# Linear attention beside a Mish layer: query exponentials normalized before they are turned, numerators without zero blocks, one load of key and value weights, a new order of steps

## Chip, cores and metric

One core of a Trainium2 chip runs the whole program. The metric is the time of one execution on the device in microseconds; 151.07 is the median of three runs of the kernel before. The engines are named as in the profile: PE (matmuls) with PEld (its weight loads), ScalarE (ACT), VectorE (DVE), GpSimd (POOL) and SyncE (SP), which here only issues DMA transfers. Each engine works through its own queue in program order and waits on semaphores of the others.

## What is computed

2048 tokens of width 448 are layer-normalized; the result goes through two branches, which are added to the input.

```python
xn = layernorm(x)
# branch A: 16 heads of width 28
q, k, v = heads(xn @ wqkv)
pq, pk = q @ w_phi, k @ w_phi                     # per head, 28 x 28
phi_q = concat(softmax(pq), softmax(-pq))         # 56 features
phi_k = concat(softmax(pk), softmax(-pk))
kv  = phi_k.T @ v                                 # per head, 56 x 28
z   = phi_k.sum(over tokens)
num = phi_q @ kv
den = phi_q @ z + 1e-6
a = heads_joined(num / den) @ wo
# branch B
h = xn @ w1 + b1                                  # width 1792
b = (h * tanh(softplus(h))) @ w2
out = x + a + b                                   # bf16
```

## The kernel before

The tokens stand in 16 tiles t of 128, worked on in 8 pairs u = t // 2. The program is a list of named steps, the table ORDER; a step appends instructions to the queues of one or more engines, and the class Program puts in the waits. The order of the table is therefore the order on each engine. The steps:

- `l...` load: x tiles (`lx0` to `lx6`), key weights (`lkm`), value weights (`lvm`), both their last 64 rows twice (`lkt`), query weights transposed by DMA (`lqT0` to `lqT3`), then `l1m`, `l1t` (W1), `l2` (W2), `lo` (Wo). Almost all go through SP's queue.
- `z12` warms PE up with 12 matmuls on zeros (L364).
- `st`, `rs`, `xn`, `xt`: the layer norm of a pair: BN statistics on VectorE (L462, L464; with b the second tile's on ScalarE), 1/sqrt on ScalarE or GpSimd (L473), the normalized tile (L497, GpSimd L492), and its transpose xnT, by PE (L505) or by a DMA transpose.
- `wtk`, `wmk`, `wmq`: w_phi is multiplied into the key weights (transposed by PE, L556, then L580) and into the query weights. For the latter VectorE first doubles the last columns of WqT (`qd`, L286).
- `v`, `k`, `q`: the three products of a pair (L423), each cut into parts A, B (6 matmuls of 64 rows by 448 columns each) and H (2). Two row halves run side by side. v is copied out; k and q leave through two exponentials on ScalarE, exp(x) and exp(-x) (L618, L680).
- `kn`: key features of a pair and a sign are normalized: reduce (L626) and reciprocal (L628) on VectorE, multiply on GpSimd (L630).
- `e`: a tile of query exponentials, not normalized, is turned into EqT by a DMA transpose. There are three buffers for them: Eq0 and two rows of actT, which the feed-forward branch writes later.
- `kv`: 32 small matmuls of a pair add phi_k^T v into one bank (L649). `kvz` copies the sum to KVT (L660), in blocks with zeros between them, and a DMA transpose makes KVZ.
- `nd`: numerators and denominators of a tile: 16 matmuls of 60 columns (L722). A product's 60 columns hold for one sign and two heads both the sum over that sign's features and, from the column of ones beside v, z and the plain sum of the exponentials. VectorE copies the two plain sums (L738), multiplies each sign's numerator by the other's sum (L742, L744), adds (L746), takes the reciprocal (L748) and multiplies (L749).
- `ot`, `wo`: the result of a pair is turned by DMA and multiplied by Wo (L845).
- `f0`, `f1`: W1 for one block of 128 hidden units and half of the tokens, 14 matmuls of 512 columns (L423), left through Mish on ScalarE (L699). `g`: W2 for a tile, 14 matmuls of 448 columns (L828), then the addition to x (L793) and the stores `sto`, `stt`.

Products that live longer than one step hold two of the eight PSUM banks, a pair of banks; a pair is opened again after its last reader, mostly ScalarE, is done. Four such pairs are in use in turn.

Of the kernel before, what the change touches and what calls it, by code (L numbers as in the profile page):

```python
# [12 lines left out]
D = 448  # L13
# [7 lines left out]
G = 4  # L21
# [6 lines left out]
NDW = 2 * (DH + 2)  # L28
# [10 lines left out]
class Program:  # L39
# [4 lines left out]
    def __init__(self, nc, es):  # L44
        self.nc = nc
        self.es = es
        self.ops = {e: [] for e in self.ENGINES}
        self.writers = {}
        self.readers = {}
        self.psum = {}  # L50
        self.n_dma = 0

    def op(self, eng, fn, r=(), w=(), dma=False, tag="", after=()):
# [84 lines left out]

def bass_parallel_sum__linear_kernel_hedgehog__dense_activation_mish__prompt_kernel(
# [8 lines left out]
pv table lx2s lba zero pm st2b lx3s lkms lps st3b lkts z12 pi b1 rs2p pw rs3a xn2d bd lx1s wtk0b lvms lx4s xn3d xt2b  # L148
wtk1b wmk0b lqT2 xt3a v2Ha wmk1a v2Ba lqT0 st1 v3Ha lqT1 lqT3 rs1a v3Aa v2Aa st4 rs4p pk v3Ba k3H lx0s k3A qd xn1d
wmq0d wmq1a k2H k3B lx6s pp k2A st5 q3A xn4d k2B q3B rs5p q2A xt1m l1ts q3H k1A q2H xn5p xt4m st0 v1Ad k1H st6 xt5m e7  # L150
rs0p q2B st7 xn0d v1Bd k1B v1Hd rs7p rs6p k4A k4H q1B k4B xn6d q1H q1A v4Ad k5H xn7d v4Hd k5A v4Bd v5Ad kn1.0 xt0m k5B
v5Bd k0B xt6m v5Hd xt7m v0Ba kn2.1 kn2.0 k0H k0A e3 k6H k6A kn0.0 e2 v6Ba l1ms k6B v0Ha kn0.1 v0Aa v6Aa v6Ha k7H k7A
q4B e6 k7B v7Aa v7Ha kn7.0 q4H q4A q6A q6H v7Ba e9 q6B kn6.0 f0.2B kn5.1 f0.0A f1.2A f0.2A f0.0H f1.2H kn6.1 e5 f1.3B
f0.2H f0.0B e12 f1.2B f1.3A kn4.1 f0.3B kn5.0 f1.3H e13 f0.3H f0.1B e4 f0.3A f0.1H f0.1A q7H q0A kn3.1 q0H kn4.0 q5B
e8 q0B q7B kv5 kn7.1 e0 kv0 kv2 q7A q5A f0.13A q5H f0.13B kv7 kv4 e10 kv6 f0.13H f0.6H f0.6A kn3.0 f0.10A f0.6B kn1.1
f0.10B kv3 kv1 ep f0.10H f1.7H f1.7A e11 f1.9A kvz f1.7B f0.12B f1.5B f0.12A f1.5H f0.5H f1.9H f0.12H l2s f1.9B f1.5A
f0.5A f1.1A nd3 f1.1B f0.5B e15 f1.0A f1.1H f1.13B f1.0H f1.13H f1.0B nd2 los f1.13A ot1m f1.8B f0.9H f1.8A f1.8H nd0
f0.11B f0.9A f0.11A f0.11H f0.7A f0.7H f0.8B nd6 e14 f0.8H f0.9B f0.7B e1 f0.8A f1.12H f1.12A f1.10A nd7 f1.10B f1.4H
f1.10H f1.12B ot3m f1.4A nd1 f1.6B f1.4B f0.4H f1.6A ot0m f0.4A wo1H f1.6H f0.4B nd4 wo1A wo3A wo1B wo3H nd5 ot2m g1
g3 g2 f1.11A f1.11H nd11 wo0B f1.11B wo3B wo0A nd13 wo0H nd10 g6 ot5m g0 g7 g11 nd12 wo2A wo5A sto1 ot6m wo5H wo2B  # L160
nd15 nd9 g10 sto0 g5 nd14 ot7m wo2H wo5B nd8 g4 g9 g14 g13 g12 g8 sto3 ot4m wo4H wo4A wo6B wo7B sto2 wo6H wo6A sto5
wo4B sto4 wo7H wob wo7A g15 stt14 sto6 stt15
# [8 lines left out]
def _kernel(es, nc, A_x, A_wqkv, A_w_phi, A_wo, B_w1, B_b1, B_w2, out):  # L171
# [43 lines left out]
    KVT = sb("KVT", [P, G, 2, 2, 64], BF16)  # L215
    KVZ = sb("KVZ", [P, 2 * G, P], BF16)
    rden = [sb(f"rden{i}", [P, H], FP32) for i in range(2)]
    Sq = [sb(f"Sq{i}", [P, 2, H], FP32) for i in range(2)]

    o_sb = [xn[i][:, :].rearrange("p (i d) -> p i d", i=2) for i in range(2)]  # L220

    def as_t(n):
        return v_flat[:, :].bitcast(FP32)[:, n * H * (DH + 1):(n + 1) * H * (DH + 1)].rearrange("p (h c) -> p h c", c=DH + 1)

    t1, t2 = [as_t(0), as_t(1)], as_t(2)
# [116 lines left out]
    def p_pads():  # L342
        for i in (1, 2, 0):
            op("POOL", lambda e, i=i: e.memset(Eq_of(i).rearrange("p i s (h n) -> p (i s h) n", n=64)[:, :, QP:64], 0.0),
               w=[("Eqp", i)] + ([(n, h) for n in ("WT", "WU") for h in range(2)] if i == 0 else []), tag=f"pp{i}")

    def p_kvt():
        op("POOL", lambda e: e.memset(KVT[:, :, :, :, :].rearrange("p g s x f -> p (g s x f)").bitcast(mybir.dt.uint32),
                                      0), w=[("KVT0",)], tag="pk3")

    def eps_rows():
        for i in range(2):
            op("DVE", lambda e, i=i: e.tensor_reduce(epsT[:, i:i + 1], ap_on(ident[:, DH + i:DH + i + 1], [[32, 4]]),
                                                          AX.X, ALU.add),
               r=[("ident",)], w=[("epsT", i)], tag=f"ep{i}")
        op("DVE", lambda e: e.scalar_tensor_tensor(epsT[:, 2:3], epsT[:, 0:1], DEN_EPS / 2, epsT[:, 1:2], ALU.mult,
                                                   ALU.add), r=[("epsT", 0), ("epsT", 1)], w=[("epsT", 2)], tag="ep2")
# [621 lines left out]
```

## Time and profile before

| | |
|---|---|
| time, median of 3 runs | 151.07 us (150.71 to 151.2) |
| profiled execution, span | 148.7 us, 3864 instructions |
| profiled execution, own time | not given beside the span |
| granted PE clock over the span | 1.000 |
| DMA traffic | 17.23 MB, mean 116 GB/s |

The page of a profile lists the busy time of each engine, then the span in 40 slices of 3.7 us with a digit of the busy share in tenths, then the chain that ended last, followed back from the last instruction to what released it. Groups of instructions are given as line, engine, operation, output from input, shape, count, then busy time in us, mean duration in ns, and the idle time of the engine before them with what ended it. A timeline or chain row begins with its start and its length in us.

### The profile page before, as it was taken

The page shows a single profiled execution, that of the slowest core. Times are in us where ns is not written, and L with a number is a line of the kernel's source. Part 1 is how long each engine was busy: PE and PEld are TensorE (multiplying, and loading weights), DVE is VectorE, ACT ScalarE, POOL GpSimd, SP SyncE. Part 2 cuts the span into 40 slices and gives each one's busy share as a digit, 9 for nine tenths or more (in the row PEclk, how much of TensorE's full clock was granted, in tenths as well). Part 3 has the DMA queues.
Part 4 walks back from the last instruction along what each step waited for, and adds up shares of the span by engine and source line. Part 5 has one row for each costly group of instructions (what it writes and reads, how often), then busy time and mean ns, then how long its engine had stood idle before and what let it go on. Part 6 is the DMA issues. An engine that isn't in the chain of part 4 may idle for free.

```text
span 148.7 us, 3864 instructions
## 1 busy us (share of the span) xinstructions
PE 144.0 (97%) x1669; PEld 74.2 (50%) x1669; DVE 102.7 (69%) x229; ACT 74.7 (50%) x91; POOL 38.9 (26%) x53
## 2 busy tenths in 40 slices
PE   6899999999999999999999999999999999999992
PEld 2365555555444555444444445545555555555561
DVE  0699898996999930407787989529983999930072
ACT  4997999779999999567747661002000000000000
POOL 4424465179999992000000000000000000000000
PEclk9999999999999999999999999999999999999999
DMA  4997997799699069499956053210013130551005
GB/s 131 245 278 216 119 185 149 126 170 344 103 188 196 14 52 132 85 239 295 195 98 125 4 62 62 43 23 0 7 37 86 35 93 0 123 127 58 4 10 175
DMA packets 39964, 17.23 MB, mean 116 GB/s; under 512 B 33932, under 2 KB 39180, under 8 KB 39948
## 3 DMA queue, kind: packets, MB, share of 16 engines
q1 hardware_dynamic: 39776, 16.89, 54.4%
q8 instruction: 13, 0.21, 0.6%
q10 hardware_dynamic: 172, 0.10, 0.2%
q14 instruction: 3, 0.02, 0.0%
HBM read 7.02 MB, written 1.84 MB: 60 GB/s over the span
## 4 chain that ended last, share of the span: by engine, by line
PE 92%; DMA 3%; DVE 2%; SPq 1%; issue 0%
PE PS L423 50%; PE PS L828 29%; PE PS L845 7%; DMA Wkv<-in_A_wqkv_dram 3%; PE PS L722 3%; PE PS L649 2%; PE PS L580 1%; DVE xn L497 1%; SPq L270 1%; PE PS L556 0%; PE PS L505 0%; DVE x_all L793 0%; DVE Eq L512 0%; DVE x_all L814 0%
## 5 line engine op out<-in xcount | busy, mean ns | idle before, releaser
L423 PE MATMUL PS<-xnT,W 64*128 64x512 bf16 x392 | 44.8, 377 | 0.0
L828 PE MATMUL PS<-W,actT 128*128 128x448 bf16 (+1 forms) x224 | 42.9, 351 | 0.0
L699 ACT ACTIVATE actT<-PS,b1T 128x1024 bf16<-128x1024 f32 x28 | 29.8, 1112 | 22.1 <-PE PS L423 22.1
L828 PEld LDWEIGHTS PS<-W,actT 128*128 128x128 bf16 x224 | 21.5, 98 | 19.8 <-issue 0.3
L423 PEld LDWEIGHTS PS<-xnT,W 64*128 64x128 bf16 x392 | 17.9, 94 | 21.9 <-PE PS L423 1.9
L630 POOL TENSOR_TENSOR actT<-actT,rSk 128x896 bf16<-128x896 bf16 x16 | 26.6, 1699 | 5.1 <-DVE rSk L628 5.1
L793 DVE TENSOR_TENSOR x_all<-PS,x_all 128x448 bf16<-128x448 f32 (+1 forms) x16 | 9.2, 613 | 15.2 <-PE PS L845 10.5
L626 DVE TENSOR_REDUCE Sk<-actT 128x32 f32<-128x896 bf16 x16 | 16.6, 1037 | 1.1 <-ACT actT L618 1.1
L618 ACT ACTIVATE actT<-PS 128x896 bf16<-128x896 f32 x16 | 13.7, 920 | 1.8 <-PE PS L423 1.7
L423 PE MATMUL PS<-Wpk,xnT 64*128 64x448 bf16 x112 | 13.2, 349 | 0.0
L423 PE MATMUL PS<-Wkv,xnT 64*128 64x448 bf16 x112 | 12.9, 349 | 0.0
L423 PE MATMUL PS<-Wpq,xnT 64*128 64x448 bf16 x112 | 12.6, 349 | 0.0
L738 DVE COPY Sq<-PS 128x16 f32<-128x16 f32 x32 | 4.0, 167 | 12.0 <-PE PS L722 12.0
L462 DVE BATCH_NORM_STATS2 stats<-x_all 128x6 f32<-128x448 bf16 x14 | 8.4, 601 | 3.4 <-DMA x_all<-in_A_x_dram 3.4
L746 DVE TENSOR_TENSOR v_all<-v_all 128x464 f32<-128x464 f32 x16 | 10.3, 641 | 0.6
L742 DVE TENSOR_TENSOR v_all<-PS,Sq 128x464 f32<-128x464 f32 x16 | 10.3, 641 | 0.5
L749 DVE TENSOR_TENSOR xn<-v_all,rden 128x448 bf16<-128x448 f32 x16 | 10.0, 625 | 0.6
L744 DVE TENSOR_TENSOR v_all<-PS,Sq 128x464 f32<-128x464 f32 x16 | 10.1, 629 | 0.0
L680 ACT ACTIVATE actT<-PS 128x896 bf16<-128x896 f32 x10 | 8.6, 930 | 0.1
L423 PEld LDWEIGHTS PS<-Wpq,xnT 64*128 64x128 bf16 x112 | 5.4, 94 | 5.0 <-ACT actT L680 0.2
L423 PEld LDWEIGHTS PS<-Wkv,xnT 64*128 64x128 bf16 x112 | 5.4, 94 | 5.1 <-ACT actT L618 0.2
L423 PEld LDWEIGHTS PS<-Wpk,xnT 64*128 64x128 bf16 x112 | 5.3, 94 | 5.1 <-issue 0.2
(83 smaller groups left out, 118.8 us busy)
## 6 DMA issues: line engine op xcount, KB each, us to landing
W<-in_B_w_dram SPq DMA_DIRECT2D x1, 1568.0 KB, 7.9
out_dram<-x_all SPq DMA_DIRECT2D x7, 224.0 KB, 2.2
W<-in_B_w_dram SPq DMA_DIRECT2D x1, 1344.0 KB, 7.0
x_all<-in_A_x_dram SPq DMA_DIRECT2D x4, 224.0 KB, 3.1
x_all<-in_A_x_dram SPq DMA_DIRECT2D x2, 448.0 KB, 4.9
Wkv<-in_A_wqkv_dram SPq DMA_DIRECT2D x2, 336.0 KB, 4.8
Wo<-in_A_wo_dram SPq DMA_DIRECT2D x2, 336.0 KB, 6.3
W<-in_B_w_dram SPq DMA_DIRECT2D x2, 224.0 KB, 4.1
```

Source lines behind the costliest of these rows:

```text
L423: ins = e.matmul(o, lhs(c, k), rhs(c, k), start=first and n == at[par][0], stop=last and n == at[par][-1])
L618: op("ACT", lambda e, s=s: e.activation(E_of(u)[:, s, :, :], two(b, D), ACT.Exp, scale=1.0 if s == 0 else -1.0), r=[pb(b), pb(b + 1)], w=[ ...
L626: op("DVE", lambda e: e.tensor_reduce(Sk[u][:, s, :], Eh(), AX.X, ALU.add), r=[("E", u, s)], w=[("Sk", u, s)], tag=f"Sk{u}.{s}")
L630: op("POOL", lambda e: e.tensor_tensor(Eh(), Eh(), ap_on(rSk[u][:, s, 0:1], [[1, 2 * H], [0, DH]]), ALU.mult), r=[("E", u, s), ("rSk", u, ...
L699: op("ACT", lambda e: e.activation(actT[:, fc, q * 1024:(q + 1) * 1024], bank(b, 2), ACT.Mish, bias=b1T[:, fc:fc + 1]), r=[("b1T",), pb(b) ...
L742: op("DVE", lambda e: e.tensor_tensor(tv(t1[i]), num(0), sx(1), ALU.mult), r=[pb(b), pb(b + 1), ("Sq", i, 1)], w=[("t1", i)], tag=f"ta{t}")
L744: op("DVE", lambda e: e.tensor_tensor(tv(t2), num(1), sx(0), ALU.mult), r=[pb(b), pb(b + 1), ("Sq", i, 0)], w=[("t2",)], tag=f"tb{t}")
L746: op("DVE", lambda e: e.tensor_tensor(t1[i], t1[i], t2, ALU.add), r=[("t1", i), ("t2",)], w=[("t1", i)], tag=f"tc{t}")
L749: op("DVE", lambda e: e.tensor_tensor(o_sb[(t // 2) % 2][:, t % 2, :].rearrange("p (h d) -> p h d", d=DH), t1[i][:, :, 0:DH], ap_on(rden[i ...
L793: op("DVE", lambda e: e.tensor_tensor(x_all[:, t, 0:n], bank(b)[:, 0:n], x_all[:, t, 0:n], ALU.add), r=[pb(b), ("x", t)], w=[("out", t)], ...
L828: ins = e.matmul(bank(b)[:, 0:width(t)], actT[:, fc, tok(t)], W2[:, fc, 0:width(t)], start=first and fc == 0, stop=last and fc == FC - 1)
L845: ins = e.matmul(bank(b)[:, 0:w], oT_of(u)[lo:hi, cc * P:(cc + 1) * P], Wo[lo:hi, cc, 0:w], start=first and n == at[par][0], stop=last and ...
```

## The change

Four things change.

1. Query exponentials are normalized like the key ones before they are turned: new steps `qn` for each tile, and the signs of a head now lie beside each other (28 + 28 of 64 columns) instead of in two halves.
2. With normalized features one product gives the sum over both signs. KVT loses its zero blocks (512 columns to 256 after the turn: 8 blocks of 128 to 4), a numerator product has 30 columns, and behind it remain a reciprocal and a multiply.
3. Key and value weights come in one load of 384 rows by 896 columns on ScalarE's queue. A load of 128 rows by 32 columns into a buffer of its own, which no instruction reads, is added.
4. The order of all steps is new.

```diff
-    KVT = sb("KVT", [P, G, 2, 2, 64], BF16)
-    KVZ = sb("KVZ", [P, 2 * G, P], BF16)
+    KVT = sb("KVT", [P, G, 2, 64], BF16)
+    KVZ = sb("KVZ", [P, G, P], BF16)
...
+    def load_kv(eng):
+        dma(eng, lambda e: e.dma_start(Wkv[:, 0:3, :], A_wqkv[0:384, D:3 * D].rearrange("(c p) f -> p c f", p=P)),
+            w=[("Wk", 0), ("Wv", 0)], tag="ldKV")
+
+    def load_first(eng):
+        dma(eng, lambda e: e.dma_start(first_rows[:], A_wqkv[0:384, D:D + 32].rearrange("(p c) f -> p c f", c=3)[:, 1, :]),
+            w=[("first",)], tag="ldfirst")
...
                 op("ACT", lambda e, s=s: e.activation(
-                    Eq_of(u)[:, :, s, :].rearrange("p i (h n) -> p i h n", n=64)[:, :, :, 0:QP],
-                    two(b, D).rearrange("p i (h n) -> p i h n", n=QP), ACT.Exp, scale=1.0 if s == 0 else -1.0),
+                    Eq_of(u)[:, :, :, s * DH:(s + 1) * DH], two(b, D).rearrange("p i (h n) -> p i h n", n=DH), ACT.Exp,
+                    scale=1.0 if s == 0 else -1.0),
...
+    def q_norm(u, i):
+        n = u % 3
+
+        def Ei():
+            return Eq_of(u)[:, i, :, 0:QP].rearrange("p h (s f) -> p h s f", s=2)
+        op("DVE", lambda e: e.tensor_reduce(Sq[u][:, i, :].rearrange("p (h s) -> p h s", s=2), Ei(), AX.X, ALU.add),
+        op("DVE", lambda e: e.reciprocal(Sq[u][:, i, :], Sq[u][:, i, :]), r=[("Sq", u, i)], w=[("rSq", u, i)],
+        op("POOL", lambda e: e.tensor_tensor(Ei(), Ei(), ap_on(Sq[u][:, i, 0:1], [[2, H], [1, 2], [0, DH]]), ALU.mult),
...
         def f(e):
-            for s in range(2):
-                for g in range(G):
-                    for r in range(2):
-                        at = (s * G + g) * NDW
-                        ins = e.matmul(bank(b + r)[:, at:at + NDW], EqT[64 * r:64 * r + QP, t, s * G + g, :],
-                                       ap_on(KVZ[64 * r:64 * r + QP, 2 * g + s, 64 * r:64 * r + 1], [[32, 2], [1, DH + 2]]),
-                                       start=True, stop=True)
+            for k in range(H // 2):
+                for r in range(2):
+                    at = 32 * (2 * r + k % 2)
+                    ins = e.matmul(bank(b + r)[:, k * NDC:(k + 1) * NDC], EqT[64 * r:64 * r + QP, t, k, :],
+                                   KVZ[64 * r:64 * r + QP, k // 2, at:at + NDC], start=True, stop=True)
...
-        for s in range(2):
-            op("DVE", lambda e, s=s: e.tensor_copy(
...
-        op("DVE", lambda e: e.tensor_tensor(tv(t1[i]), num(0), sx(1), ALU.mult), r=[pb(b), pb(b + 1), ("Sq", i, 1)],
-        op("DVE", lambda e: e.tensor_tensor(tv(t2), num(1), sx(0), ALU.mult), r=[pb(b), pb(b + 1), ("Sq", i, 0)],
-        op("DVE", lambda e: e.tensor_tensor(t1[i], t1[i], t2, ALU.add), r=[("t1", i), ("t2",)], w=[("t1", i)],
...
+        op("DVE", lambda e: e.reciprocal(rden[:, t, :].rearrange("p (r k) -> p r k", r=2),
+                                         ap_on(bank(b)[:, DH:DH + 1], [[TCW, 2], [NDC, H // 2]])),
+        op("DVE", lambda e: e.tensor_tensor(
+            o_sb[(t // 2) % NXN][:, t % 2, :].rearrange("p (r k d) -> p r k d", r=2, d=DH), num(0, DH),
+            ap_on(rden[:, t, 0:1], [[H // 2, 2], [1, H // 2], [0, DH]]), ALU.mult),
...
-pv table lx2s lba zero pm st2b lx3s lkms lps st3b lkts z12 pi b1 rs2p pw rs3a xn2d bd lx1s wtk0b lvms lx4s xn3d xt2b
+lx3a zero pm lx1s lkva table pp lkta st3b pi pw lps lbs rs3a lx2s lqT2 st1 lqT0 rs1a xn3d z12 xn1x bd wtk0b xt3d wtk1b
...
+q6A f0.3A q6H f0.0B f0.3B f0.1H lfrs kn3.1 f0.0A f0.1B f0.3H e8 f0.0H f1.2B f0.1A qn4.1 f1.2A f1.2H f1.1A e4 f1.1H
```

The step `xn1x` normalizes one tile on VectorE and the other on ScalarE; `lfrs` is the added small load. Where the order moves instructions that matter for the time:

SyncE's queue of transfers at the start of the program before (x tiles, key weights, w_phi, the weights' last rows, value weights, query weights):

```order
L270 DMA x_all<-in_A_x_dram 128x896 x2
L273 DMA Wkv<-in_A_wqkv_dram 128x3x448
L293 DMA Wraw<-in_A_w_phi_dram 112x4x28
L278 DMA Wkv<-in_A_wqkv_dram 64x896 x2
L270 DMA x_all<-in_A_x_dram 128x896
```

ScalarE's queue at the same place now, followed by its part of the statistics of one tile:

```order
L304 DMA x_all<-in_A_x_dram 128x896
L316 DMA Wkv<-in_A_wqkv_dram 128x3x896
L352 ACT_TABLE_LOAD
L312 DMA Wkv<-in_A_wqkv_dram 64x896 x2
L466 ACTIVATE junk,mv<-x_all 128x448
```

One x tile pair and all key and value weights have moved from SyncE's queue to ScalarE's; SyncE keeps the other x tiles, w_phi, b1 and the query weights.

VectorE's queue now from the first normalized pair (xn3) to the copy that doubles WqT (L328; before, L286):

```order
L520 TENSOR_SCALAR xn3<-x_all,mv,rstd 128x384
L502 SCALAR_TENSOR_TENSOR shift<-mv,rstd 128x1
L520 TENSOR_SCALAR xn1<-x_all,mv,rstd 128x448
L535 COPY Eq0<-PS 112x512
L535 COPY xnT<-PS 128x896
L535 COPY Eq0<-PS 112x512
L535 CAST b1T<-PS 128x14
L475 BN_STATS stats<-x_all 128x6
L477 BN_AGGR mv<-stats 128x2
L475 BN_STATS stats<-x_all 128x6
L477 BN_AGGR mv<-stats 128x2
L535 CAST Wpk<-PS 128x448 x2
```

L328 follows this row. Two statistics pairs precede it here where four stood just ahead of it before, and three tiles' statistics have been done ahead of xn3.

PE's queue around the last key-value step, before (L649 the key-value steps, L722 the first numerators):

```order
L423 MATMUL PS<-xnT,W 128x512 x28
L649 MATMUL PS<-actT,v_all 30x56 x64
L423 MATMUL PS<-xnT,W 128x512 x72
L722 MATMUL PS<-KVZ,EqT 128x60 x16
L423 MATMUL PS<-xnT,W 128x512 x36
```

and now (L672 and L756):

```order
L435 MATMUL PS<-xnT,W 128x512 x96
L672 MATMUL PS<-actT,v_all 30x56 x96
L435 MATMUL PS<-xnT,W 128x512 x44
L756 MATMUL PS<-KVZ,EqT 128x30 x16
L435 MATMUL PS<-xnT,W 128x512 x12
```

The matmuls between the last key-value step and the first numerators fell from 72 to 44. GpSimd's queue ahead of that last step, where before only the key multiplies L630 stood, is now mixed (L718 query, L653 key; the digit is the pair):

```order
L653 TENSOR_TENSOR actT<-actT,rSk6 128x896
L718 TENSOR_TENSOR actT<-actT,Sq7 128x16x56
L653 TENSOR_TENSOR actT<-actT,rSk5 128x896 x2
L653 TENSOR_TENSOR actT<-actT,rSk7 128x896
L653 TENSOR_TENSOR actT<-actT,rSk6 128x896
L718 TENSOR_TENSOR actT<-actT,Sq5 128x16x56
```

The last rSk6 row is what the last key-value step waits for; eleven L718 rows stand ahead of it, five behind.

232 lines of the change are left out of this document (122 added, 110 removed).

## Prediction

> **What bounds the kernel now.** I read the page first, for which engine is full and whether it stays full; then the chain that ended last; then what PE waited for.
>
> ```profile
> PE 144.0 (97%) x1669; PEld 74.2 (50%) x1669; DVE 102.7 (69%) x229; ACT 74.7 (50%) x91; POOL 38.9 (26%) x53
> PE   6899999999999999999999999999999999999992
> PEclk9999999999999999999999999999999999999999
> ```
>
> The matmul engine is busy in every slice but the first three and the last, at full granted clock. The chain says the same (start, length, what; the count after x is of matmuls):
>
> ```profile
> 1.72 4.95 DMA Wkv<-in_A_wqkv_dram
> 6.72 0.67 PE PS L556 x8
> ...
> 10.42 3.32 PE PS L423 x34
> ...
> 14.64 36.25 PE PS L423 x370
> 50.89 0.88 PE PS L649 x96
> ...
> 59.18 7.90 PE PS L423 x72
> 67.08 0.22 PE PS L722 x16
> ...
> 88.60 1.89 PE PS L845 x20
> ...
> 142.98 2.42 PE PS L828 x14
> ...
> 145.42 0.56 DVE x_all L793
> 145.98 0.19 DVE x_all L814
> ```
>
> From 10.42 to 145.40 one PE piece follows another. Only three things can move the time: how many microseconds of matmuls there are, when the unbroken run begins, and any wait that breaks it. Up to the run, PE waited only for the key weights:
>
> ```profile
> PE PS L556 <- DMA Wkv<-in_A_wqkv_dram: 0.4, 1, 0.4
> ```
>
> The sum is made against the profiled span, 148.7 us. No separate time of that execution is given; the median of the three runs, 151.07, stands 2.37 above the span, and I carry these 2.37 unchanged. 0.3% is 0.45 us, about what a measurement here can tell from no change; a time between 150.62 and 151.52 counts as the same.
>
> **Numerators without zero blocks.** Still 256 matmuls, of 30 columns instead of 60.
>
> ```profile
> L722 PE MATMUL PS<-KVZ,EqT 56*128 56x60 bf16 x256 | 6.0, 187 | 0.0
> L649 PE MATMUL PS<-actT,v_all 128*30 128x56 bf16 x256 | 2.6, 192 | 0.0
> 145.34 0.57 PE L810 MATMUL PS<-W,actT 128*128 128x64 bf16 x14
> ```
>
> One step costs 0.22 us (chain, L722 x16): 8 pairs, the two row halves side by side, 27 ns a pair. Next to it: 14 matmuls of 64 columns take (0.57 - 0.19) / 13 = 29 ns each, and the L649 ones, 56 columns and four side by side, 0.88 us for 24 sets in the chain, 37 ns a set with the changes between steps. No row steps faster than 27, so the trace cannot tell what holds a pair at 27 ns: 60 columns at 2.4 columns per ns (25 ns; 64 would be 26.7, in line with 29), or the two 128-column weight loads. From the first, 30 columns give 12.5 + 2.5 = 15 ns, saving 16 x 8 x 12 ns = 1.5 us; from the second nothing. I take 26 ns, just under the shortest step shown: **-0.1 us**, ends -1.5 and 0.
>
> The Trainium skill, TensorE: Matmul & The Clock Gate, section "Wait — 56ns, not 53.3ns?", says that start-to-start never drops below about 25 ns however few columns. By that the pair saves 2 ns and the sum would be -0.3; no run here shows 30 columns.
>
> **What the numerator step leaves on VectorE.** Two copies and three multiply-adds per token tile go; reciprocal and final multiply stay.
>
> ```profile
> L746 DVE TENSOR_TENSOR v_all<-v_all 128x464 f32<-128x464 f32 x16 | 10.3, 641 | 0.6
> L742 DVE TENSOR_TENSOR v_all<-PS,Sq 128x464 f32<-128x464 f32 x16 | 10.3, 641 | 0.5
> L744 DVE TENSOR_TENSOR v_all<-PS,Sq 128x464 f32<-128x464 f32 x16 | 10.1, 629 | 0.0
> L738 DVE COPY Sq<-PS 128x16 f32<-128x16 f32 x32 | 4.0, 167 | 12.0 <-PE PS L722 12.0
> ```
>
> 34.7 us of VectorE work after 67 us disappear, but PE waits for none of it: its chain there is unbroken. Worth 0.
>
> **Query normalization.** 16 reduces and reciprocals on VectorE and 16 multiplies on GpSimd come before the turns. The key side has the same sizes:
>
> ```profile
> L626 DVE TENSOR_REDUCE Sk<-actT 128x32 f32<-128x896 bf16 x16 | 16.6, 1037 | 1.1 <-ACT actT L618 1.1
> L628 DVE RECIPROCAL rSk<-Sk 128x32 f32<-128x32 f32 x16 | 5.7, 353 | 0.6
> 31.71 24.88 POOL L630 TENSOR_TENSOR actT<-actT,rSk 128x896 bf16<-128x896 bf16 x15 [0.76 <-DVE rSk L628]
> 18.45 1.73 POOL L492 TENSOR_SCALAR xn<-x_all,rstd,shift 128x448 bf16<-128x448 bf16 x3 [0.38 <-DVE shift L485]
> ```
>
> That is about 1.35 us a pair on VectorE (22 in all) and 24.88 / 15 = 1.66 on GpSimd (27 in all), hidden beside matmuls as long as their consumers come later. The new GpSimd order puts 11 query multiplies among the 16 key ones before the last L672 step (kv6). GpSimd then needs 27 x 1.66 + 1.1 (the xn6 half) + 0.9 (rstd) = 46.8 us. It starts when the first reciprocal is done: VectorE, after doubling WqT at about 12.0, runs xn2 (0.9), 8 BN pairs (0.73 each), small ones (0.7) and the first reduce (1.35), to 20.8. So kv6's factor is ready at 67.6. PE reaches kv6 after 314 matmuls of 448 columns (1.89 / 20 = 94.5 ns), 208 of 512 (7.90 / 72 = 110 ns), 16 small ones and 7 key-value steps (0.29 each), 55.5 us from 11.95, at 67.4. The cover is gone to within 0.2 us; I book **+0.2**, ends 0 and +2 (the multiply's three-level operand is not in the trace; a tenth slower would be +1.9).
>
> **The turn of KVZ.** After the last kv step the program now has 44 matmuls of 512 columns where it had 72.
>
> ```profile
> 59.26 1.84 DVE L660 TENSOR_SCALAR KVT<-PS,epsT 30x224 bf16<-30x224 f32 x4 [5.97 <-PE PS L649]
> KVZ<-KVT SPq DMA_TRANSPOSE x1, 3.2
> ```
>
> The way to the first numerator is 1.84 + 3.2 + some 0.1 of handover = 5.1 us; 44 x 110 ns cover 4.8. Before, 72 covered 7.9. **+0.3**, ends 0 (the turn is of half the size) and +0.8.
>
> **Banks.** ScalarE empties the banks at 0.83 and 1.01 us an operation:
>
> ```profile
> 15.54 3.43 ACT L618 ACTIVATE actT<-PS 128x896 bf16<-128x896 f32 x4
> 43.08 4.13 ACT L699 ACTIVATE actT<-PS,b1T 128x1024 bf16<-128x1024 f32 x4 [0.21 <-PE PS L423]
> ```
>
> ((3.43 - 0.92) / 3 and (4.13 - 1.11) / 3.) Followed along the new order between 12 and 56 us, each pair is emptied 0.1 to 0.7 us before PE reopens it: 22 exponentials and 6 value copies against 23.5 us of PE. Normalized query rows are overwritten only after multiply and turn, which the order leaves just enough time for. Booked 0, ends 0 and +0.8.
>
> **The start.** The loads move to two queues, and the key weights' 336 KB become part of 672. PE's wait for Wkv ended at 6.68; its 12 warm-up matmuls end at 6.2, so an earlier landing is worth at most 0.5. What ends last in the new start is VectorE's queue. Ahead of the copy that doubles WqT, which the query-weight product waits for, stand:
>
> ```profile
> 3.43 0.63 DVE L462 BATCH_NORM_STATS2 stats<-x_all 128x6 f32<-128x448 bf16 x1 [3.43 <-DMA x_all<-in_A_x_dram]
> 6.42 0.90 DVE L497 TENSOR_SCALAR xn<-x_all,mv,rstd 128x448 bf16<-128x448 bf16 x3
> 7.41 0.42 DVE L512 COPY Eq<-PS 112x512 bf16<-112x512 bf16 x1
> 9.59 0.61 DVE L512 CAST Wpk<-PS 128x448 bf16<-128x448 f32 x1
> 13.13 0.23 DVE L286 COPY WqT<-WqT 128x256 bf16<-128x256 bf16 x1
> ```
>
> five BN pairs (3.7), four passes of xn (1.4), two WT copies (0.8), the whole xnT copy (0.7, scaled by width), b1T (0.2), two Wpk casts (1.2), the copy itself (0.2): 8.2 us from 3.43, thus 11.7 if never starved; I take 11.95. By then PE has done 22 of the value matmuls; in before, at 11.95, it had done 2 and then 1.53 us of the run, 18. Four matmuls ahead: **-0.4 us**. If the 672 KB land at 7.5 instead of 6.4, the copy ends near 12.7 and it is +0.4; if all goes smoothly, -0.6.
>
> On this the Trainium skill, DMA: Bandwidth & Descriptors, section "Issuing engines are not separate DMA queues", says that a second queue only saves issue time. By it the two loads share the engines and the landing would tend to the later end, +0.4; no row of before has two large loads on both queues.
>
> The small first load is issued in the middle of the program, and nobody reads it: 0. The tail (g15, its two additions, two stores) is the same: 0.
>
> **Sum.** -0.1 + 0.2 + 0.3 + 0 - 0.4 = 0.0: span 148.7, time 151.07, **151.1 us**. The terms' likely ends put this case between 150.5 and 151.8.
>
> **The rivals.**
> *Numerators stream.* If columns alone set the 27 ns, the pair falls to 15 and the sum to -1.4: 149.7 us. For it: steps of 64 and 60 columns differ by about the columns between them. Against it: nothing shorter than 27 ns is shown.
> *GpSimd becomes the bound.* A query multiply over 16 x 2 blocks may take longer than the 1.66 of 32 plain blocks. From 1.66 on, each 0.1 us costs 11 x 0.1 = 1.1 us of PE waiting at kv6, since PE is in order. At 1.83: +1.9 instead of +0.2: 152.8 us, slower. For it: the order leaves 0.2 us there, and GpSimd's work goes from 39 to some 66 us. Against it: the same count of elements and type.
> *The change does not do what it says at the start.* The small load is not first and the key weights come with 336 KB more; landing at 7.5 gives +0.4 for -0.4: 151.9 us. For it: Wkv took 4.95 us with less ahead. Against it: its rows are twice as long and one queue is free of it.
>
> **Chances.** Forecast 0.36; numerators stream 0.32; GpSimd 0.18; late weights 0.14. Faster by over 0.3%: all of the second and 0.08 of the forecast, 0.40. Slower: GpSimd, 0.06 of late weights and 0.04 of the forecast, 0.28. Same: 0.32. The range reaches from a little below the streaming case, 149.4, to the GpSimd case, 152.8. The forecast's own is 150.5 to 151.8.
>
> **What would show it.** A numerator step of 16 matmuls in the chain near 0.21 us (0.12 if they stream). A wait of PE before the first L756, released by the KVZ transfer, of about 0.3. A wait of L672 for GpSimd of 0.2 or less; 1 us or more means the second rival, and the mean of L718 would then exceed 1700 ns. The query-weight product beginning near 12.0, released by VectorE's copy. Scattered waits for ScalarE between 12 and 60 us that sum to over 1 us would make the forecast wrong from a side I booked at nothing.

## The result and the profile after

The changed kernel took 155.72 us, the median of four executions: 154.8, 155.6, 155.83 and one of 299.46, whose 448-column matmuls came every 417 ns instead of 189, for a reason that the record doesn't show. The kernel before took 151.12 beside it: ratio 1.0289, interval 1.0253 to 1.0326. Medians are over all executions of a kernel; ratios and intervals leave out those that took over 1.5% more than its fastest, such as the one of 299 us. That one was the profiled execution, so the profile read here is of the same kernel in run e1 (155.04 us, ratio 1.0291, interval 1.0223 to 1.0359). The change costs about 4 us where no change was forecast.

First the page of e1: busy time by engine, then the slices.

```profile
PE 144.5 (95%) x1669; PEld 74.7 (49%) x1669; DVE 92.0 (60%) x177; ACT 75.5 (49%) x92; POOL 66.6 (44%) x71
PE   7779998978999997999999999999999999999993
DVE  0789999999999999996776644230305600100371
POOL 6303599799699999999992000000000000000000
PEclk9999999999999999999999999999999999999999
```

PE has as many matmuls as before and nearly the same busy time, at full clock. It is no longer busy in every slice: holes stand at 24 to 35 us, near 58, and a deeper one at the start. VectorE is full from slice 4 to slice 18, GpSimd almost from 6 to 21. Next, what PE waited for (total, times, longest), without the wait ahead of its warm-up matmuls (1.0 here, 1.4 before):

```profile
PE PS L435 <- ACT actT L702: 1.5, 2, 0.9
PE PS L579 <- DMA Wkv<-in_A_wqkv_dram: 1.0, 1, 1.0
PE PS L435 <- ACT v_all L533: 0.8, 1, 0.8
PE PS L528 <- DVE xn L520: 0.6, 1, 0.6
PE PS L435 <- DMA xnT<-xn: 0.5, 1, 0.5
PE PS L435 <- DVE v_all L535: 0.3, 1, 0.3
PE PS L528 <- ACT xn L515: 0.2, 1, 0.2
```

These sum to 4.9 us; before, one wait of 0.4 was listed. That is the loss. Five waits behind the start carry 3.1 of it: 0.52 at 24.4, 0.78 at 31.0, 0.57 at 34.6, 0.30 at 52.3 and 0.92 at 58.1. The chain says who was late:

```profile
10.55 0.54 DVE stats L475
...
24.84 1.06 issue
25.90 2.65 DVE xn L520 x4
...
35.60 2.57 DVE xn L520 x3
...
51.55 0.96 DVE v_all L535
52.50 0.05 issue
52.55 4.54 PE PS L435 x46
```

Before, the chain was PE's own from 10.42 on. Now it runs almost wholly through VectorE from 10.38 to 52.50, and three pieces of it are too long. They stand in VectorE's timeline, and what GpSimd does at the same time in its own (start, length):

```profile
24.78 1.20 DVE L502 SCALAR_TENSOR_TENSOR shift<-mv,rstd 128x1 f32<-128x1 f32 x1
25.90 2.65 DVE L520 TENSOR_SCALAR xn<-x_all,mv,rstd 128x448 bf16<-128x448 bf16 x4
35.52 2.65 DVE L520 TENSOR_SCALAR xn<-x_all,mv,rstd 128x448 bf16<-128x448 bf16 x3
```

```profile
22.62 3.35 POOL L718 TENSOR_TENSOR actT<-actT,Sq 128x896 bf16<-128x896 bf16 x2
25.93 1.69 POOL L718 TENSOR_TENSOR Eq<-Eq,Sq 128x896 bf16<-128x896 bf16 x1
27.61 1.31 POOL L510 TENSOR_SCALAR xn<-x_all,rstd,shift 128x64 bf16<-128x64 bf16 x2
34.46 3.39 POOL L653 TENSOR_TENSOR actT<-actT,rSk 128x896 bf16<-128x896 bf16 x2
```

One number per partition took 1.20 us and was done at 25.98, when GpSimd's second multiply was done (25.97). The first of the four passes then ended at 27.75, just behind the third multiply (27.62); the other three ran in 0.9 us. Their usual lengths are 0.15 for the single number and, in run e5 below, 1.19 for the four passes. These VectorE operations stood still while a multiply ran.

The third piece, at 35.52, is another case. The multiplies beside it are key ones (L653), which the kernel before had too, and no wait of PE follows it. In run e4 below, where no query multiply is left, it is nearly as long beside them, VectorE's line first:

```profile
32.39 2.32 DVE L520 TENSOR_SCALAR xn<-x_all,mv,rstd 128x448 bf16<-128x448 bf16 x3
31.01 3.39 POOL L653 TENSOR_TENSOR actT<-actT,rSk 128x896 bf16<-128x896 bf16 x2 [1.68 <-DVE rSk L651]
```

The Trainium skill, SBUF — State Buffer, section "Who interferes with whom", says that VectorE's fast copies and scalar passes share a pair of ports with GpSimd, and that whoever starts first holds them for its whole instruction. It says too that a VectorE instruction with two inputs in SBUF contends with a GpSimd instruction that reads SBUF; the single number (from mv and rstd) is such a one. The 1.20 and the 2.65 agree, and the reduces beside the same multiplies, 1.03 to 1.07 us, agree too: the page exempts them. One thing differs: three of those bf16 passes ran at their usual length beside GpSimd's own scalar passes (L510, 27.61 to 28.92). The operation on a single number was held by such a pass as well: at 20.14 it took 0.37 and ended at 20.51, when a pass of L510 ended (20.50).

### The profile page after: what moved, and what is told of

It is laid out like the page before. It is cut to its first block, busy times and chain, and to the rows that moved or that the text cites. A ratio compares the mean times of both kernels' runs of the same rounds, so it can differ in the third digit from the quotient of the medians.

```text
span 297.6 us, 3825 instructions
## 1 busy us (share of the span) xinstructions
PE 294.4 (99%) x1669; PEld 114.1 (38%) x1669; DVE 91.7 (31%) x177; ACT 78.0 (26%) x92; POOL 66.9 (22%) x71
## 4 chain that ended last, share of the span: by engine, by line
PE 97%; DMA 1%; POOL 0%; SPq 0%; issue 0%; DVE 0%; POOLq 0%
PE PS L435 54%; PE PS L850 30%; PE PS L867 8%; DMA Wraw<-in_A_w_phi_dram 1%; PE PS L756 1%; PE PS L603 1%; PE PS L672 1%; PE PS L579 1%; PE PS L528 1%; POOL Wbd L562 0%; PE PS L830 0%; SPq L304 0%; DVE x_all L834 0%; PE PS L827 0%; PE PS L728 0%
## 5 line engine op out<-in xcount | busy, mean ns | idle before, releaser
L435 PE MATMUL PS<-xnT,W 64*128 64x512 bf16 x392 | 94.7, 671 | 0.0
L850 PE MATMUL PS<-W,actT 128*128 128x448 bf16 (+1 forms) x224 | 91.0, 617 | 0.0
L850 PEld LDWEIGHTS PS<-W,actT 128*128 128x128 bf16 x224 | 33.1, 149 | 56.3 <-issue 56.0
L435 PEld LDWEIGHTS PS<-xnT,W 64*128 64x128 bf16 x392 | 28.3, 141 | 52.3 <-issue 50.4
L653 POOL TENSOR_TENSOR actT<-actT,rSk 128x896 bf16<-128x896 bf16 x16 | 26.8, 1700 | 22.6 <-DVE rSk L651 22.6
L435 PE MATMUL PS<-Wpk,xnT 64*128 64x448 bf16 x112 | 27.1, 618 | 0.0
L435 PE MATMUL PS<-Wpq,xnT 64*128 64x448 bf16 x112 | 26.8, 608 | 0.0
L435 PE MATMUL PS<-Wkv,xnT 64*128 64x448 bf16 x112 | 26.3, 609 | 0.0
L718 POOL TENSOR_TENSOR actT<-actT,Sq 128x896 bf16<-128x896 bf16 x10 | 16.9, 1698 | 14.1 <-DVE Sq L716 14.1
L649 DVE TENSOR_REDUCE Sk<-actT 128x32 f32<-128x896 bf16 x16 | 16.6, 1038 | 2.1 <-ACT actT L641 2.1
L718 POOL TENSOR_TENSOR Eq<-Eq,Sq 128x896 bf16<-128x896 bf16 x6 | 10.3, 1714 | 25.4 <-DVE Sq L716 23.5
L714 DVE TENSOR_REDUCE Sq<-actT 128x32 f32<-128x896 bf16 x10 | 10.5, 1050 | 12.6 <-ACT actT L702 12.6
L867 PE MATMUL PS<-Wo,Wkv 64*128 64x448 bf16 x56 | 12.7, 597 | 0.0
L756 PEld LDWEIGHTS PS<-KVZ,EqT 56*128 56x128 bf16 x256 | 8.2, 112 | 9.0 <-issue 8.7
```

Of the source, the lines that this page charges most:

```text
L435: ins = e.matmul(o, lhs(c, k), rhs(c, k), start=first and n == at[par][0], stop=last and n == at[par][-1])
L649: op("DVE", lambda e: e.tensor_reduce(Sk[u][:, s, :], Eh(), AX.X, ALU.add), r=[("E", u, s)], w=[("Sk", u, s)], tag=f"Sk{u}.{s}")
L653: op("POOL", lambda e: e.tensor_tensor(Eh(), Eh(), ap_on(rSk[u][:, s, 0:1], [[1, 2 * H], [0, DH]]), ALU.mult), r=[("E", u, s), ("rSk", u, ...
L714: op("DVE", lambda e: e.tensor_reduce(Sq[u][:, i, :].rearrange("p (h s) -> p h s", s=2), Ei(), AX.X, ALU.add), r=[("Eq", n, i, s) for s in ...
L718: op("POOL", lambda e: e.tensor_tensor(Ei(), Ei(), ap_on(Sq[u][:, i, 0:1], [[2, H], [1, 2], [0, DH]]), ALU.mult), r=[("Eq", n, i, s) for s ...
L756: ins = e.matmul(bank(b + r)[:, k * NDC:(k + 1) * NDC], EqT[64 * r:64 * r + QP, t, k, :], KVZ[64 * r:64 * r + QP, k // 2, at:at + NDC], st ...
```

## The experiments

T1 was that PE's clock is released later, T2 that PE waits for others. Behind the first three runs T2 became T3 (GpSimd's multiplies hold up VectorE and the turns) against T4 (VectorE is simply full). Medians in us, the ratio with its interval to the kernel before, run beside them (151.04 to 151.36):

| run | edit of the changed kernel | median | ratio |
|---|---|---|---|
| e1 | none | 155.04 | 1.0291 (1.0223 to 1.0359) |
| e2 | 20 warm-up matmuls | 155.28 | 1.0275 (1.0244 to 1.0306) |
| e3 | numerators stream 60 columns | 155.70 | 1.0299 (1.0254 to 1.0344) |
| e4 | no query multiplies | 152.02 | 1.0062 (1.0040 to 1.0083) |
| e5 | one multiply later | 153.93 | 1.0193 (1.0142 to 1.0245) |
| e6 | key weights alone first | 154.92 | 1.0256 (1.0229 to 1.0282) |
| e7 | W2, Wo later | 161.54 | 1.0698 (1.0645 to 1.0751) |
| e8 | first loads as before | 154.91 | 1.0214 (1.0157 to 1.0272) |
| e9 | no small load | 155.34 | 1.0264 (1.0226 to 1.0302) |
| e10 | no query normalization | 151.64 | 1.0026 (1.0003 to 1.0048) |
| e11 | order of before | 179.62 | 1.1892 (1.1846 to 1.1937) |
| e12 | two turns earlier | 154.45 | 1.0193 (1.0158 to 1.0227) |
| e13 | e5 and e12 | 153.91 | 1.0160 (1.0098 to 1.0223) |
| e14 | e13, passes earlier | 154.38 | 1.0196 (1.0154 to 1.0239) |
| e15 | e14, loads of e8 | 154.10 | 1.0183 (1.0138 to 1.0228) |
| e16 | e13, W1 and pair 5 earlier, 16 warm-up | 153.35 | 1.0132 (1.0074 to 1.0190) |
| e17 | as e16, loads of e8, 12 warm-up | 155.37 | 1.0185 (1.0078 to 1.0292) |

Differences of less than 0.5 us are not read.

### The clock, the numerators (e1 to e3)

e1:

> The changed kernel again, for an undisturbed profile: a span near 153. T1 (the matmul clock is released later than before): the row of granted clock or the pace of the first matmuls shows it; matmuls of 448 columns take about 190 ns instead of 94.5 for some 4 to 8 us near the start, and once the clock is full PE is unbroken, with less than 1 us of waiting. T2 (PE waits for others): full clock from the first value matmul on, and waits that sum to 3 to 5 us, in few places: kv6 for GpSimd (1 to 2), the first numerators for the turn of KVZ (0.3 to 1), exponentials of ScalarE and the transposed x between 12 and 60 us (1 to 3).

e2:

```diff
-xn3d z12 xn1x
+xn3d z12 z8 xn1x
```

> The changed kernel with 8 more warm-up matmuls on zeros behind the first 12, nothing else changed. T1: PE is busy without a gap until its first real matmul and the clock is full then: 2 to 4 us faster than the changed kernel (about 152). T2: the first real work is held by the 8 matmuls or not at all: equal or up to 1 us slower (155.5 to 157).

e3:

```diff
-ins = e.matmul(bank(b + r)[:, k * NDC:(k + 1) * NDC], EqT[64 * r:64 * r + QP, t, k, :],
-               KVZ[64 * r:64 * r + QP, k // 2, at:at + NDC], start=True, stop=True)
+ins = e.matmul(bank(b + r)[:, k * 2 * NDC:(k + 1) * 2 * NDC], EqT[64 * r:64 * r + QP, t, k, :],
+               ap_on(KVZ[64 * r:64 * r + QP, k // 2, at:at + 1], [[0, 2], [1, NDC]]), start=True, stop=True)
```

> The changed kernel with each numerator matmul streaming its 30 columns twice (60 columns, as many as before), nothing else changed. If a pair of numerator matmuls is held by something other than columns (my -0.1): a step stays at 0.21 to 0.22 us and the time at 155.7 within 0.3. If columns set it (the rival that numerators stream): the step goes from 0.12 to 0.22 and the time up by 1.5 us. T1 and T2 say nothing on it.

T1 falls as the main cause: the clock was full in e1's profile, and more warm-up brought nothing. T2 stands, with other places than I named: nothing at kv6, nothing at the first numerators. For the numerators, a step in the chain of e1, then of e3:

```profile
78.27 0.19 PE PS L756 x16
```

```profile
77.90 0.22 PE PS L756 x16
```

In e3 the product writes its 30 columns twice, and the readers of the bank step by 60 columns likewise. By the starts of the matmuls a step takes 0.205 us with 30 columns and 0.223 with 60: a pair follows every 25 ns, or every 27 to 28. So half the columns take some 3 ns off a pair, not 12; columns are not what mainly holds it. 16 steps save about 0.3 us, which the times of e3 don't resolve.

### GpSimd's multiplies (e4, e5, e10)

e4 leaves the 16 query multiplies out:

```diff
-        op("POOL", lambda e: e.tensor_tensor(Ei(), Ei(), ap_on(Sq[u][:, i, 0:1], [[2, H], [1, 2], [0, DH]]), ALU.mult),
```

> The changed kernel without the 16 multiplies of GpSimd that normalize the query exponentials (left out; the sums and reciprocals of VectorE stay). Theory T3: those multiplies hold VectorE's normalizing passes up (in the changed kernel three of them took 1.20, 1.85 and 1.67 us in place of 0.15 to 0.38) and delay the query turns, so PE's four waits between 30 and 60 us (0.78, 0.57, 0.30, 0.92) go: 2.0 to 2.6 us faster than the changed kernel, about 152.7. Rival T4: VectorE is simply full (22 us of new sums and reciprocals before 52 us); these stay, so the waits stay and the time is within 0.6 of 155.0.

e5, with the step qn cut into sums (qs) and multiply (qm):

```diff
-v4Ba xt7m qs3.1 qm3.1 xn6y q4A xn0d v4Aa
+v4Ba xt7m qs3.1 xn6y q4A xn0d qm3.1 v4Aa
```

> The changed kernel with one multiply of GpSimd (of query pair 3, second tile) moved behind VectorE's normalizing passes of pairs 6 and 0; sums and reciprocals stay where they are. T3: GpSimd's run of multiplies is over at about 26.0 instead of 27.6, the pass of pair 0 ends 1.3 us earlier, its turned copy lands at 30.3 instead of 31.6, and the waits of 0.78 at 31 us and 0.57 at 35 us go: 0.8 to 1.3 us faster, about 154.0. T4: VectorE has the same work before that pass: unchanged within 0.4.

e10 leaves out sums, reciprocals and multiplies:

> The changed kernel with the whole query normalization left out: sums, reciprocals and multiplies. Against the run without the multiplies (152.0) it tells what VectorE's 22 us of sums and reciprocals cost. T3 (GpSimd's multiplies were nearly all of it): 151.4 to 152.0. T4 (VectorE full): 150.5 to 151.2, since the waits that were left (0.58 at 24, 0.28 at 33) go too.

e4 was 3.0 us faster than e1, so T3 holds and T4 falls. What PE still waits for in e4:

```profile
PE PS L579 <- DMA Wkv<-in_A_wqkv_dram: 1.0, 1, 1.0
PE PS L435 <- DMA xnT<-xn: 0.6, 1, 0.6
PE PS L754 <- DVE xn L764: 0.3, 1, 0.3
PE PS L435 <- ACT actT L702: 0.3, 1, 0.3
```

The waits of 0.8, 0.3 and 0.9 are gone and that of 0.57 is 0.3. That of 0.5 near 24 is still there (0.58), so it is not theirs. The 3.0 are more than the 2.0 to 2.6 expected, and not all of them are the multiplies': in the profiles 0.6 of 3.1 is there before the first query multiply runs (PE's 61st matmul starts at 11.49 in e1, at 10.93 in e4), which leaves about 2.5. With the sums gone as well (e10) the time is 0.4 lower, too little to read: VectorE's 22 us of new work, which fill it to 52 us, cost next to nothing by themselves.

e5 shows the mechanism with all the work kept. Its VectorE, then its GpSimd:

```profile
24.13 1.20 DVE L502 SCALAR_TENSOR_TENSOR shift<-mv,rstd 128x1 f32<-128x1 f32 x1
25.25 1.19 DVE L520 TENSOR_SCALAR xn<-x_all,mv,rstd 128x448 bf16<-128x448 bf16 x4
```

```profile
25.43 1.38 POOL L510 TENSOR_SCALAR xn<-x_all,rstd,shift 128x64 bf16<-128x64 bf16 x2
26.78 3.35 POOL L724 TENSOR_TENSOR Eq<-Eq,Sq 128x896 bf16<-128x896 bf16 x2
```

The four passes take 1.19 instead of 2.65 and end at 26.4 instead of 28.55. The time falls by 1.1, as T3 had it; in the profiles it is 1.5, of which 0.7 stand before 11.5 us (the 61st matmul starts at 10.84). The wait at 31 is gone, but that at 35 came out at 1.0 instead of 0.57, since its own cause, below, was untouched.

That wait at 31 also teaches how the list is to be read. It is put down to ScalarE's copy of v, which ended last before PE went on. But v0 needs the turned copy of pair 0, and that was issued at 28.58 in e1, right behind the blocked pass. It landed at 31.62, and PE went on at 31.75.

```profile
28.58 1.23 SPq L540 DMA_TRANSPOSE xnT<-xn  x1
29.85 1.31 SPq L723 DMA_TRANSPOSE EqT<-actT  x1
```

When e5 ended the passes earlier, the wait went with them.

### Loads (e6 to e9)

e6:

```diff
-lx1s lkva table pp lkta st3b
+lx1s lkma table pp lkta lvma st3b
```

> The changed kernel with the key weights loaded first by themselves (336 KB) and the value weights by a load of their own behind the two tails. If the joint load of 672 KB is what makes the start late (late weights, and x3 with it): the key weights land near 6.3 instead of 7.1, PE's three waits before 10 us sum to 0.7 to 1.2 instead of 1.8, and the time falls by 0.5 to 1.0 unless VectorE's queue behind it takes it back (then it stays within 0.4 of 155.0).

e7 moves `l2a` and `los` behind `kvz f1.11H`:

> The changed kernel with the loads of W2 and Wo (1568 and 784 KB) issued behind the turn of KVZ instead of at 53.5 us. The wait of 0.92 at 58 us ends with ScalarE's exponentials of query pair 0, which waited for their buffer, whose turn landed 4.56 us after its issue instead of 3.1, beside these loads. If the loads do that: the turn lands at about 55.7, the wait goes, and the time falls by 0.9 (154.1). If the late issue of the turn (GpSimd's multiplies) sets it: less than 0.3.

e8:

```diff
-lx3a zero pm lx1s lkva table pp lkta st3b pi pw lps lbs rs3a
+lx3s zero pm lx1s lkms table pp lkta st3b pi pw lps lbs rs3a lvma
```

> The changed kernel with the first loads as before the change had them: the rows of pair 3, those of pair 1 and the key weights (336 KB alone) one behind the other on SP's queue, the value weights on ScalarE's queue later. The rows of pair 3 land at 3.4 instead of 4.5, so VectorE's unbroken queue (10.4 to 52.5 in the changed kernel) begins about 1.0 earlier. If that queue sets PE's waits, the time falls by 0.8 to 1.3 (about 154.0). If the start is taken back by waits behind it that have other causes: less than 0.4.

e9 drops `lfrs`:

> The changed kernel without the small load of 128 short rows in the middle of the program, which nobody reads. In three of seven profiles the turned copy of pair 5, issued right ahead of it, landed 4.6 to 4.8 us after its issue instead of 3.0, together with the small load, and PE waited 0.5 to 1.8 us near 41. If the small load does that: the copy lands in 3.0 us always, no wait near 41, and the median falls by 0.2 to 0.6; if it does not: within 0.2 of 155.0 and a late copy still in some profile.

e6: the key weights landed at 6.0, but PE's waits before 10.1 us still sum to 1.6, and the time didn't move. x3, which starts VectorE, landed at 4.53 as in e1. In e8 it came 0.9 earlier (VectorE's first row at 3.65 instead of 4.54), and the four times spread from 153.5 to 157.3, too wide to tell 0.5 from 1.3. e7 was a miss with a price: the turn at 52.8 took 4.2 us without any load beside it, for 4.6 with them, so the loads hardly slow it, and at their new place they held up five query turns. The longest of PE's waits in e7:

```profile
PE PS L756 <- DMA EqT<-Eq: 4.8, 1, 4.8
```

e9 refutes my reading of the late copy at 41: without the small load it still landed after 4.6 us. The small load costs nothing.

### The order (e11 to e17)

e11 takes ORDER of before, with `qnU.0 qnU.1` put behind the last part of each `qU`:

> The new numerators and the query normalization in the order and with the loads of before, each normalization put right behind its query product. GpSimd then has 28 multiplies of 1.70 us ahead of the last key-value step, which PE reaches at about 59; started near 20 they end at 68 to 72. If GpSimd's 1.70 us a multiply is the price of this change in any order, PE waits 6 to 10 us there and the time is 157 to 161. If the new order itself is the loss: about 151.

```profile
PE PS L672 <- POOL actT L653: 13.4, 4, 4.9
PE PS L435 <- DVE v_all L535: 9.5, 2, 8.2
```

The loss, 28 us, is three times the most that was forecast: GpSimd's queue costs 13.4, and VectorE's queue ahead of a value copy another 9.5, for which I had no term. Of the two orders the new one is much the better for these numerics; the steps `qnU` were tried at this one place of the old order only.

e12, then e13 with the edit of e5 as well:

```diff
-xt0m q4B k7B v7Aa v7Ha st5 rs5p k4B qs2.1 qm2.1 v7Ba e3 kn1.0
+e3 xt0m q4B k7B v7Aa v7Ha st5 rs5p k4B qs2.1 qm2.1 v7Ba kn1.0
...
-e7 v0Aa
+e7 e5 v0Aa
...
-v5Bd e5 k6H
+v5Bd k6H
```

> The changed kernel with two query turns earlier in SP's queue, nothing else: the second turn of pair 1 ahead of the turned copy of pair 0 (its data is ready at 26.0, it was issued at 29.85), and the second turn of pair 2 behind those of pair 3 (ready at 34.5, issued at 52.56). If it is the place in SP's queue that keeps ScalarE's exponentials of pairs 4 and 5 from their buffers: the waits of 0.57 at 35 and 0.92 at 58 go and the time falls by 1.0 to 1.5 (about 153.7). If the multiplies of GpSimd keep them: unchanged within 0.4.

> The two turns of the run before and the one GpSimd multiply moved behind the normalizing passes, together. Separate causes add: 155.0 - 1.1 - 1.2 = 152.7. One cause seen twice: about 153.7.

e14, beside the edits of e13 (`xn5d` and `xt5m` also leave their old places), and e15 with the loads of e8:

```diff
-rs7p xn4p st6
+xn4p rs7p st6
...
-xn7y qs1.0 qm1.0 rs6a
+qs1.0 xn7y qm1.0 rs6a
...
-st5 rs5p k4B
+st5 rs5a xn5d k4B
...
-xt6m
+xt6m xt5m
```

> As the run before, and the normalizing passes of pairs 4, 7 and 5 earlier: GpSimd does pair 4 ahead of the scale of pair 7, VectorE does pair 5 before the multiplies of the first keys begin (its scale on ScalarE), and the turned copy of pair 5 follows that of pair 6. If the blocked passes are the cause (1.8 us of blocking in pair 5's, the late copy of pair 4): the waits near 24, 41 and 52 (0.5, 0 to 1.8, 0.3) go and the time falls by another 0.6 to 1.0, to about 151.9. If those waits only move: as the run before.

> As the run before, with the first loads as before the change (pair 3's rows first, key weights alone). If the start is a cause of its own: another 0.6 to 1.2 less, near 151.0, as fast as the kernel before or faster. If it is taken back behind: as the run before within 0.4.

e16: e13, the last two edits of e14, `l1ts` behind `l1ms`, and `z12 z4`; e17: the same with `z12` and the loads of e8.

> The moved multiply, the two moved turns, the early passes of pair 5 with its turned copy behind that of pair 6, the two tails of W1 loaded right behind its main part, and 4 more warm-up matmuls. The waits that came up in the place of those removed (1.2 to 1.8 near 37 to 42: the turned copy of pair 5 and the tails of W1) go, and no execution shows half a clock at the start. If each wait has a cause of its own: 152.2 to 152.8. If the late copies only move on to the next place: 153.5 to 154.5, as the four runs before.

> As the run before, but with 12 warm-up matmuls and with the first loads as before the change. The start then begins VectorE's queue 1.0 earlier: 151.2 to 151.9 if it is a cause of its own; as the run before if it is taken back by waits behind it.

In e12 the waits at 35 and 58 are gone. These two came from the place of two finished turns in SP's queue: the exponentials of a later pair could not overwrite their buffer, which shows in ScalarE's timeline of e1 as idle time (in brackets) ahead of them:

```profile
33.36 1.73 ACT L702 ACTIVATE actT<-PS 128x896 bf16<-128x896 f32 x2 [1.63 <-PE PS L435]
...
57.19 1.73 ACT L702 ACTIVATE actT<-PS 128x896 bf16<-128x896 f32 x2 [1.94 <-PE PS L435]
```

The brackets name PE, whose products were done earlier (30.97 for the first, about 56 for the second); the turn issued at 29.85 landed at 33.2, that issued at 52.56 at 57.12. In e5, whose order of turns is that of e1, the list names the turn itself:

```profile
32.13 1.73 ACT L702 ACTIVATE actT<-PS 128x896 bf16<-128x896 f32 x2 [1.18 <-DMA EqT<-actT]
```

But 1.8 came up near 41 (the turned copy of pair 5, issued at 38.3, landed at 42.3), and only 0.6 of the expected 1.0 to 1.5 was won. In e13 it was 1.6 at the same place, put down to that copy. In e14 pair 5 was early, and the next thing was late: W1's tails, queued on SP behind the turns, as e15's waits name it:

```profile
PE PS L436 <- DMA W<-in_B_w_dram: 1.5, 1, 1.5
```

So in e14 and e15 the waits only moved. With W1's tails moved up too (e16) the waits shrank to 2.6 us in the profile, and the median to 153.35, 1.7 below e1; the passes that had 5.7 us in e1 between 18 and 52 us have 2.5. First e1, then e16:

```profile
L520 DVE TENSOR_SCALAR xn<-x_all,mv,rstd 128x448 bf16<-128x448 bf16 (+2 forms) x8 | 5.7, 761 | 0.0
```

```profile
L521 DVE TENSOR_SCALAR xn<-x_all,mv,rstd 128x448 bf16<-128x448 bf16 (+2 forms) x8 | 2.5, 361 | 1.2 <-ACT rstd L494 1.2
```

It missed its 152.2 to 152.8 by half a microsecond, and one of its four executions still lost part of the clock (157.64, mean 0.989). e17 missed its 151.2 to 151.9 by far, at 155.37. No version beat the kernel before.

With the waits shorter a bound comes into sight that the lists don't name: the last key multiply of GpSimd, which kv6 needs. It ended at 72.78 in e1 and at 72.88, 71.13 and 74.00 in e12, e16 and e17, and PE began kv6 0.18, 0.06, 0.06 and 0.05 us behind it. In the last three kv6 came some 0.3 us later than the pace of the other kv steps. In e4, without query multiplies, that multiply ended 1.9 us before kv6.

The start stays open: the old loads brought nothing clear in e8, e15 or e17; in e17 PE waited 1.9 for the key weights and 1.0 for the first normalized tile.

## Why the prediction was wrong

- **The step that failed** stands in the paragraph on query normalization: the new sums and multiplies are "hidden beside matmuls as long as their consumers come later". I priced GpSimd by its own queue alone, and asked only whether its last multiply comes before kv6. The multiplies also stop scalar passes of VectorE, and these feed the turned copies that PE reads 3 us later. Against the usual 0.15 and 1.19 the two long pieces of e1 beside query multiplies lost 1.05 and 1.46 us. The third lost 1.76 (0.89 in e16), but beside key multiplies: in e4 it stayed, and it cost PE nothing in e1. Leaving the query multiplies out gave 3.0 us back (155.04 to 152.02) of the 3.75 that part e1 from the kernel before beside it (151.29), some 2.5 of them behind the first such multiply. These hold two effects: the stopped passes (e5, which moves one multiply out of their way, gains 1.1), and turns that the multiplies make late, with what stands behind them in SP's queue (the waits of 0.57 and 0.92, see the overwritten rows below). No run measured the two apart. Neither a term nor a rival held this; it could have been read from VectorE's timeline of before, where a scalar operation on one number a partition took 1.65 us, inside the stretch of key multiplies that the prediction quotes for its price alone:

```profile
51.64 1.65 DVE L356 SCALAR_TENSOR_TENSOR epsT<-epsT 128x1 f32<-128x1 f32 x1
```

- **GpSimd as the bound at kv6**, +0.2 and the rival of +1.9: the multiplies follow each other every 1.66 us, as estimated, and e1 lists no wait for GpSimd at kv6. The price was right and the times weren't: the last key multiply ended at 72.78, not 67.6, since the first multiply began at 22.62, not 20.8, and GpSimd idled on the way. PE was as late (72.96, not 67.4); where the order made PE quicker (e12, e16, e17) it met this bound. In the rival's case of 1.83 the sum is 0.2 + 11 x 0.17 = 2.1, not 1.9.
- **Normalized rows overwritten** only after their turn, "which the order leaves just enough time for": wrong. The waits of 0.57 and 0.92 are this, and e12 removed both, though another of 1.8 came up. I had followed when a turn can start, but not where it stands in SP's queue.
- **Banks**, 0 with an end of +0.8: the waits put down to ScalarE sum to 2.3, over the 1 us that the prediction named as a sign against it, but none of them came from the pace at which it empties banks; it was waiting for buffers or a turned copy itself.
- **Numerators**, -0.1 at 26 ns: direction right and size near; 25 ns measured, -0.3. The streaming rival (15 ns) is refuted. The Trainium skill's floor of about 25 ns (TensorE: Matmul & The Clock Gate, "Wait — 56ns, not 53.3ns?") agrees with these 25, if it is counted from pair to pair: the two matmuls of a pair start 3 ns apart. The -0.3 that the prediction works out from it is the term; the sum by it would have been -0.2.
- **KVZ**, +0.3: no wait. The turn landed 2.4 us after its issue (75.36), not 3.2: my lower end was right.
- **The start**, -0.4: wrong sign. VectorE began at 4.54, not at the 3.43 of before, and the copy that doubles WqT came at 12.98, not 11.95. x3 landed at 4.52; its load starts together with another x load, and where it was alone at the head of its queue (e8) it landed at 3.62. The 672 KB are not the cause: with 336 KB in their place (e6) x3 landed at 4.53. PE waited 1.8 before 10 us, 1.3 more than before. Part of that is the stopped passes again: the first normalizing pass took 1.03 us in e1 (from 6.89), beside two multiplies of w_phi on GpSimd (6.46 to 7.54) and the clearing of KVT, and PE waited 0.59 for it. In e4 these multiplies ran at 5.67 to 6.74, the pass took 0.40, and that wait is not there. The late-weights rival is near the truth here (the 672 KB landed at 7.1), but e6 had them at 6.0 and was no faster, and e10, with the same loads and no normalization, is within 0.5 of the kernel before. What the start costs by itself stays open.
- **VectorE's relief** behind 67 us: worth 0, as said. **The small load**: 0, as e9 shows.
- **2.37 us** between span and time was carried from two different executions; in the runs here time and span of one execution lie 2.0 apart, so the profiled span of 148.7 was a quick one, by some 0.3 us.

## What to carry to other kernels

Work put on GpSimd is not free for VectorE: look at which short VectorE operations stand beside GpSimd's two-input operations, and keep those that feed a transfer out of their way. When the order changes, follow the issuing queue too: a finished transfer behind one that waits frees its buffer late. A wait removed in a chain this tight brings the next one up, so a repair is worth its size only when all that is queued behind is early as well.

## What the runs showed of the hardware

**Half a clock for 3.41 us.** In e8 PE waited 3.0 us near 57; then the clock was halved for one stretch of 3.41 us. Windows of e8 (from and to, length; busy time of PE, PEld, VectorE, ScalarE, GpSimd with counts; granted clock, DMA share, GB/s):

```profile
57.00:60.70 3.70, 0.77 (x8) 0.41 (x10) 3.60 (x6) 2.55 (x4) 3.70 (x3) 1.00 1.11 325
60.70:64.10 3.40, 3.40 (x167) 2.13 (x164) 1.79 (x4) 3.38 (x4) 3.40 (x3) 0.50 0.58 169
```

The same happened at the start of e12, where PE was busy for 1.68 of 3.41 us. Below, windows of e12 and, for comparison, of e1, busy for 1.81, where the clock held:

```profile
4.84:8.26 3.42, 1.68 (x17) 0.95 (x16) 3.27 (x12) 2.65 (x10) 1.33 (x3) 1.00 1.13 278
8.26:11.67 3.41, 3.41 (x30) 2.24 (x28) 2.61 (x8) 2.85 (x5) 0.00 (x0) 0.50 1.06 292
```

```profile
6.43:9.84 3.41, 1.81 (x26) 1.56 (x27) 3.33 (x10) 2.16 (x7) 1.33 (x3) 1.00 1.29 236
```

At the start, the five profiles (e7, e12, e13, e14, e17) with PE busy for under half of the first stretch at full clock got half of it in the next; the others with a record of the clock, from 0.51 busy, did not. In mid-program three stretches of 0.41 to 0.48 in e11 kept the clock, so the share alone is not the rule. The four executions of e2 all kept the full clock (mean 1.0); of the 64 of the other runs, without e7 and e11, 25 have a mean of 0.978 to 0.989, and were mostly 0.5 to 1.5 us longer, a few 2 to 4. So T1 had a share after all, in some executions. The Trainium skill, TensorE: Matmul & The Clock Gate, section "What's actually happening", has a free-running window of 3413 ns and asks for an idle window; the 3.41 agree, but a stretch half busy was enough here.

**Late turns beside instruction loads.** In e1's list of transfer queues stands

```profile
q8 instruction: 13, 0.21, 0.6%
```

13 blocks of 16 KB, 0.9 to 1.5 us each. The turns and turned copies of e1 between 25 and 70 us that had no such block in flight landed 3.0 to 3.5 us after their issue, but for one of 4.1; those issued at 51.3, 52.6 and 66.2, with a block that began while they were under way, took 4.9, 4.6 and 4.3. The late copy of pair 5 had one as well (4.6 us in e9, with a block from 40.2 on). But in e1 that copy, issued at 38.2 with a block from 40.6 on, took 3.0, and a turn of e12, issued at 32.6, took 4.7 with no block in flight. It was seen, not tried: no run moved the blocks.
